# Block-sparse attention scores: both heads of a pair in the two halves of TensorE's rows, the block mask as a product of its own

## The chip, the cores and the metric

The program runs on one core of one Trainium2 chip. The metric is the device time of one execution, in microseconds (us). The engines named below are TensorE (PE in the profile; its weight loads are PEld), VectorE (DVE), ScalarE (ACT), GpSimd (POOL) and the sync engine (SP), which here only issues DMAs.

## What is computed

There are 4 batches, 8 heads, 768 positions and a head size of 64. Every query attends to its own block of 64 keys and to the 3 of the 12 blocks with the highest gate scores, causally. The output of attention, `x` of 768 x 512 per batch, goes through a two-dimensional Fourier transform (the real part is added), a normalisation and a two-layer network.

```python
k_rep = k.reshape(B, H, n_blocks, 64, D).mean(axis=3)
gate_scores = np.where(causal, np.einsum('bhsd,bhnd->bhsn', q, k_rep), -1e9)
top_idx = np.argsort(gate_scores, axis=-1)[..., -3:]
# mask: the 3 blocks of top_idx and the own block, and key position <= query position
scores = np.where(mask, scale * q @ k.T, -1e9)
x = softmax(scores) @ v
...
u = x + real(fft(fft(x, axis=1), axis=2))
un = (u - mean(u)) / sqrt(var(u) + 1e-6)
out = u + relu(un @ w_ch1) @ w_ch2
```

## The kernel before

Heads are taken two at a time: 16 pairs, `kk` from 0 to 15, four to a batch. Queries and keys lie transposed, head size on the partitions, and scores are computed with keys on the partitions and queries along the columns, so that the exp of a score tile is at once the weights of the product with v.

**Stages of a pair.** `stage_A` (called twice by `stage_AA`, first for k, then for q; line 247) transposes 128 x 128 tiles of both heads on TensorE in f32. VectorE copies q to `qt` (line 264) and sums k by blocks into `kr12` (line 270); GpSimd casts each head's q from `qt` into rows 0 to 63 of `qg[e]` (line 267); ScalarE casts each head's k into rows 0 to 63 of `kI[e]` (line 282; for pairs 0 to 6 one of the four casts is VectorE's, line 280). `stage_B` (line 287) computes the gate scores (ten f32 products `g`), then VectorE finds the eight largest of each row (`max`), marks the blocks below the third largest and takes the own block out (lines 294 to 306). `stage_C` (line 308) transposes these marks with five products `gt`, whose weights have 44 columns, and VectorE copies them into rows 64 to 75 of `qg[0]` and `qg[1]`, two copies of 12 x 640. Rows 64 to 75 of `kI[e]` hold a constant, `IndN`: -60000 where the key lies in block n, else 0. So one product over 76 rows gives score plus block mask.

**Sections.** `stage_S(kk, e, s)` (line 334) computes one of three sections of one head's scores: 896 columns in two or three products (the list `SECS`) into `sp`, a tile of two PSUM banks named `sc` with two buffers. For pairs below `EARLY` = 7 it also adds a triangle of -60000 (`ltri`, line 348) to each diagonal tile by a product with the identity; for later pairs VectorE multiplies the result by a 0/1 triangle instead (line 355). ScalarE takes the exp of 896 columns at once into `ptl` (line 349). `stage_AV` (line 357) multiplies with v in 21 products of 65 columns, VectorE divides by the sum into `x` (lines 374 and 375), and for the second head of a pair sums and differences for the transform follow: `fs` on GpSimd (on VectorE for the last pair of a batch), then `ft`, `fo`, `fc` (lines 383 to 407).

**The rest of a batch.** `stage_S1` (products `za`, `ya`, lines 416 to 424) and `stage_S2` (`mx`, lines 448 to 459) transform, `stage_N` normalises, `stage_T` transposes (`unt`, line 506), `stage_M1` (`ha`, `hb`, line 522) and `stage_M2` (`ch`, line 536) are the network; M1 and M2 make up most of TensorE's work.

**The order** of TensorE's and GpSimd's instructions is the order in which the program issues them. It is written out by hand in the loop over pairs (lines 653 to 689): six sections a pair, one after another, each followed by a slot of `filler` and one of the other stages. `filler` takes units of the rest of earlier batches from a queue, by a planner's clock (`feed.now`) in which each unit has a cost: chain units (S1, S2, T) are taken in order, each once the clock stands a given gap past the end of the one before it, bulk units (M1, M2) at any time; line 573 shares the work out evenly. A section advances the clock by at least `PACE` = 1.4. A batch's S1 follows 3.5 after the second `stage_AV` of its fourth pair. VectorE, ScalarE and the DMA queues have their instructions ordered by the compiler's scheduler.

Of the kernel before, what the change touches and what calls it, by code (L numbers as in the profile page):

```python
# [118 lines left out]
def kernel(  # L119
# [9 lines left out]
    nc = tc.nc  # L129
# [55 lines left out]
    kI_t = [[const([128, S], F16, f"kI_{e}_{sl}") for sl in range(3)] for e in range(2)]  # L185
    v16_t = [const([128, 2, NST, 66], F16, f"v16_{sl}") for sl in range(4)]
    qg_t = [[const([128, S], F16, f"qg_{e}_{sl}") for sl in range(3)] for e in range(2)]
    warm = const([128, 512], F16, "warm")
    kr24_t = [const([128, 2 * NB], FP, f"kr24_{sl}") for sl in range(2)]
    gmp_t = [const([128, NST - 1, 2, 32], F16, f"gmp_{sl}") for sl in range(2)]  # L190
# [56 lines left out]
    def stage_A(kk, who, g):  # L247
        d = P[kk]
        src = d["qn"] if who == 0 else d["kn"]
        if who == 0 and g == 0:  # L250
            d["qt"] = apool.tile([128, S], FP, tag="qT32", name=f"qT32_{kk}")
            d["qg"] = [qg_t[e][kk % 3] for e in range(2)]
        if who == 1 and g == 0:
            d["kI"] = [kI_t[e][kk % 3] for e in range(2)]
            d["kr12"] = spool.tile([128, NB], FP, tag="kr12", name=f"kr12_{kk}", bufs=2)
            d["kr24"] = kr24_t[kk % 2]
# [6 lines left out]
        if who == 0:  # L263
            nc.vector.tensor_copy(out=d["qt"][:, cols], in_=flat)  # L264
            if g == 1:
                for e in range(2):
                    nc.gpsimd.tensor_copy(out=d["qg"][e][0:64, :],  # L267
                                          in_=d["qt"][64 * e:64 * e + 64, :])
        else:
# [7 lines left out]
            for e in range(2):  # L277
                dst, src_ = d["kI"][e][0:64, cols], flat[64 * e:64 * e + 64]
                if kk < EARLY and g == 1 and e == 1:
                    nc.vector.tensor_copy(out=dst, in_=src_)  # L280
                else:
                    nc.scalar.copy(out=dst, in_=src_)  # L282
# [4 lines left out]
    def stage_B(kk):  # L287
# [11 lines left out]
        for st in range(NG):  # L299
            for e in range(2):  # L300
                nc.vector.max(out=mx8[:, st, e, :], in_=gsb[:, st, e, :])  # L301
        gm = gmp[:, :, :, 0:NB]
        nc.vector.tensor_tensor(out=gm, in0=gsb,
                                in1=mx8[:, :, :, 2:3].to_broadcast([128, NG, 2, NB]),
                                op=mybir.AluOpType.is_lt)
        nc.vector.tensor_tensor(out=gm, in0=gm, in1=oth24[:, 1:NST, :, :], op=MULT)

    def stage_C(kk):
        d = P[kk]
        gt = pst([44, NG, 128], f"gt_{kk}", dtype=F16)  # L310
        for st in range(NG):
            nc.tensor.transpose(gt[0:44, st, :],  # L312
                                d["gmp"][:, st, :, :].rearrange("p e n -> p (e n)")[:, 0:44], id16)
        for e in range(2):
            nc.vector.tensor_copy(out=d["qg"][e][64:64 + NB, 128:S],
                                  in_=gt[32 * e:32 * e + NB].rearrange("p a c -> p (a c)"))
# [17 lines left out]
    def stage_S(kk, e, s):  # L334
        d = P[kk]
        if s == 0:
            d.setdefault("pt", {})[e] = apool.tile([128, 3 * SEC], F16, tag=f"ptl{e}",
                                                   name=f"ptl_{kk}_{e}")
        pt = d["pt"][e]
        sp = pst([128, 1024], f"sc_{kk}_{e}_{s}", tag="sc", bufs=2)  # L340
        by_pe = kk < EARLY
        for (jt, a0, a1, co) in SECS[s]:
            diag = by_pe and a0 == 128 * jt
            nc.tensor.matmul(sp[:, co:co + (a1 - a0)],  # L344
                             d["kI"][e][0:76, 128 * jt:128 * (jt + 1)],
                             d["qg"][e][0:76, a0:a1], start=True, stop=not diag)
            if diag:
                nc.tensor.matmul(sp[:, co:co + 128], id16, ltri, start=False, stop=True)  # L348
        nc.scalar.activation(out=pt[:, SEC * s:SEC * (s + 1)], in_=sp[:, 0:SEC], func=AF.Exp,  # L349
                             scale=0.125)  # L350
        if s == 2 and not by_pe:
            um = ut01.rearrange("p (o c) -> p o c", o=1).to_broadcast([128, 3, 128])
            for dg in (pt.rearrange("p (t c) -> p t c", t=3)[:, :, 0:128],
                       pt[:, 384:].rearrange("p (t c) -> p t c", t=3)[:, :, 384:512]):
                nc.vector.tensor_tensor(out=dg, in0=dg, in1=um, op=MULT)
# [190 lines left out]
    def queue_batch(b, start):  # L546
        last = start
        units = []
        for dt in (1, 0):
            last = Unit(lambda dt=dt: stage_S1(b, dt), S1_COST, last, 3.5 if dt == 1 else 0.0)  # L550
# [48 lines left out]
    PACE = 1.4  # L599
    with tc.manual_schedule(engines={mybir.EngineType.PE, mybir.EngineType.Pool}):  # L600
# [14 lines left out]
        for sl in range(3):  # L615
            for e in range(2):
                nc.gpsimd.dma_start(kI_t[e][sl][64:64 + NB, :], dr["IndN"].ap())
        nc.gpsimd.dma_start(ut01, dr["ut01"].ap())
        for e in range(2):
            for sl in range(3):  # L620
                nc.gpsimd.memset(qg_t[e][sl][64:64 + NB, 0:128], 0.0)
# [31 lines left out]
        for kk in range(NK):  # L653
            for p in range(6):
                t_in = feed.now
                main(stage_S, 0.39, kk, p // 3, p % 3)
                filler(kk, 2 * p)
                if p == 0 and kk + 2 < NK:
                    load_v(kk + 2)
                    main(stage_AA, 0.7, kk + 2, 1)  # L660
                if p == 1 and kk > 0:
                    main(stage_AV, 0.65, kk - 1, 1)
                    after_av(kk - 1)
                if p == 2:
                    if kk + 2 < NK:
                        main(stage_AA, 0.7, kk + 2, 0)
                        cast_v(kk + 2)
                    if kk == 0:
                        stage_W(4)
# [55 lines left out]
```

## Time and profile before

The times of three runs were 346.15 (median), 346.09 and 347.31 us. One further execution was profiled: it took 346.12 us, 344.3 us from its first to its last instruction (the span).

| | |
|---|---|
| profiled execution, its span | 346.12 us, 344.3 us |
| mean granted TensorE clock | 0.979 |
| ScalarE: exps of sections, line 349 | 96 x 917 ns, 87.1 us busy |
| TensorE: products of sections, line 344 | 256, 55.7 us busy; weight loads 24.5 us |
| TensorE: triangles, line 348 | 84 x 222 ns |
| ScalarE and VectorE: casts of k, lines 282 and 280 | 57 x 473 ns and 7 x 560 ns |
| GpSimd: casts of q, line 267 | 32 x 849 ns |
| VectorE: copies of the marks, line 315 | 32 x 484 ns |
| VectorE: own block out of the marks, line 306 | 16 x 217 ns |
| TensorE: gate products, line 291 | 160 x 271 ns |

A group of the profile is named by line, engine, operation and tiles (out<-in), with its count; busy time counts overlapping instructions once, and the mean is that of one instruction from start to end. TensorE's products overlap, so that the distance of their starts, which the timeline shows, is what one costs in a row of them, not its own length.

### The profile page before, as it was taken

What the parts mean: (1) busy time and instruction counts of PE and PEld (TensorE: products, weight loads), DVE (VectorE), ACT (ScalarE), POOL (GpSimd) and SP (SyncE); (2) the same over time, 40 slices, a digit from 0 to 9 for tenths busy, and PEclk for the clock granted to TensorE, in tenths of its full rate; (3) what the DMA queues carried; (4) which work ended last, traced back from release to release, by engine and by line L of the source; (5) the groups of instructions that cost most, each with busy time, mean ns of one, the idle gap of its engine ahead of it and who ended that gap; (6) DMA issues with size and microseconds to landing.
All of it is one profiled execution on the core that took longest, in us unless ns stands there. A gap on an engine that the chain in (4) does not pass through costs nothing.

```text
span 344.3 us, 6929 instructions
## 1 busy us (share of the span) xinstructions
PE 320.4 (93%) x2688; PEld 210.2 (61%) x2688; DVE 229.1 (67%) x701; ACT 172.7 (50%) x259; POOL 93.5 (27%) x177
## 2 busy tenths in 40 slices
PE   7899994998899989999999989899999999899995
PEld 3577772886766666566566766556666655456442
DVE  2788889788565779887566688986544868533211
ACT  3177885497874853454375653442566210344000
POOL 8435664244543020342215030161012100200000
PEclk9999998799699999999999999999999999999999
DMA  9999999966498440433523000011000011100021
GB/s 173 197 211 208 261 183 219 147 143 138 80 172 144 82 93 17 107 107 89 143 48 74 20 2 30 32 44 51 32 0 2 5 58 61 62 2 0 32 89 64
DMA packets 85312, 31.18 MB, mean 91 GB/s; under 512 B 77736, under 2 KB 81136, under 8 KB 85280
## 3 DMA queue, kind: packets, MB, share of 16 engines
q1 hardware_dynamic: 79984, 25.88, 33.2%
q0 software_dynamic: 3552, 4.40, 8.1%
q10 hardware_dynamic: 1744, 0.46, 0.7%
q8 instruction: 21, 0.34, 0.4%
q14 instruction: 11, 0.09, 0.1%
HBM read 28.63 MB, written 6.29 MB: 101 GB/s over the span
## 4 chain that ended last, share of the span: by engine, by line
PE 74%; DVE 12%; ACT 4%; POOL 4%; issue 3%; DMA 2%; ACTq 0%; POOLq 0%; DVEq 0%
PE ch L536 21%; PE ha L522 15%; PE hb L522 8%; PE sc L344 8%; PE g L291 5%; PE av L370 5%; PE tp L259 3%; ACT kI L282 2%; DVE kr L270 2%; DVE mx L301 2%; DMA qn<-in_q_dram 2%; PE gt L312 1%; PE ya L424 1%; PE mx L448 1%; DVE bst L461 1%
## 5 line engine op out<-in xcount | busy, mean ns | idle before, releaser
L349 ACT ACTIVATE ptl<-sc 128x896 f16<-128x896 f32 x96 | 87.1, 917 | 51.9 <-PE sc L344 42.1
L536 PE MATMUL ch<-w_sb,hT 128*128 128x512 f16 x384 | 91.2, 379 | 1.3 <-DVE u L539 1.2
L522 PEld LDWEIGHTS <-w_sb 128*128 128x128 f16 x512 | 48.8, 98 | 35.7 <-issue 0.7
L522 PE MATMUL ha<-unT,w_sb 128*128 128x512 f16 x256 | 65.7, 379 | 0.1
L344 PE MATMUL sc<-qg,kI 76*128 76x512 f16 (+3 forms) x256 | 55.7, 309 | 4.1 <-ACT ptl L349 4.0
L536 PEld LDWEIGHTS <-hT 128*128 128x128 f16 x384 | 36.1, 97 | 36.8 <-issue 1.4
L525 ACT ACTIVATE hT<-ha 128x512 f16<-128x512 f32 x64 | 38.1, 597 | 30.7 <-PE ha L522 30.7
L527 DVE TENSOR_SCALAR hT<-hb 128x256 f16<-128x256 f32 x64 | 26.9, 422 | 36.1 <-PE hb L522 36.1
L522 PE MATMUL hb<-unT,w_sb 128*128 128x256 f16 x256 | 38.4, 273 | 0.3 <-ACT unT L509 0.3
L383 POOL TENSOR_TENSOR fs<-x 128x384 f16<-128x384 f16 x12 | 11.2, 929 | 100.2 <-DVE x L375 100.2
L344 PEld LDWEIGHTS <-kI 76*128 76x128 f16 x256 | 24.5, 101 | 19.4 <-issue 2.9
L282 ACT CAST kI<-tp 64x384 f16<-64x384 f32 x57 | 27.0, 473 | 11.7 <-DVE kr L270 10.7
L267 POOL CAST qg<-qT 64x768 f16<-64x768 f32 x32 | 27.2, 849 | 19.7 <-DVE qT L264 18.7
L539 DVE TENSOR_TENSOR u<-ch,u 128x512 f32<-128x512 f32 x24 | 16.5, 688 | 21.6 <-PE ch L536 21.3
L370 PE MATMUL av<-v,ptl 128*128 128x65 f16 x672 | 26.2, 195 | 0.0
L370 PEld LDWEIGHTS <-ptl 128*128 128x128 f16 x672 | 24.8, 98 | 2.1 <-issue 0.2
L497 ACT ACTIVATE x<-u,nmr,rstd 128x512 f16<-128x512 f32 x12 | 8.9, 803 | 26.8 <-POOL nmr L490 26.8
L270 DVE TENSOR_REDUCE kr<-tp 128x6 f32<-128x384 f32 x32 | 17.0, 546 | 7.0 <-PE tp L259 6.9
L291 PEld LDWEIGHTS g<-kr,qT 128*128 128x128 f32 x160 | 20.5, 200 | 1.3 <-issue 0.3
L291 PE MATMUL g<-kr,qT 128*128 128x24 f32 x160 | 20.6, 271 | 0.0
L348 PE MATMUL sc<-ltri,id 128*128 128x128 f16 x84 | 18.6, 222 | 0.0
L375 DVE TENSOR_TENSOR x<-av,rcp 128x384 f16<-128x384 f32 x32 | 17.8, 557 | 1.0
(91 smaller groups left out, 406.5 us busy)
## 6 DMA issues: line engine op xcount, KB each, us to landing
vn<-in_v_dram SPq DMA_DIRECT2D x32, 192.0 KB, 3.6
out_dram<-u SPq DMA_DIRECT2D x24, 256.0 KB, 2.0
kn<-in_k_dram SPq DMA_DIRECT2D x30, 192.0 KB, 4.0
qn<-in_q_dram SPq DMA_DIRECT2D x30, 192.0 KB, 4.1
w_sb<-in_moe_w_ch_dram POOLq DMA_DIRECT2D x8, 256.0 KB, 6.9
w_sb<-in_moe_w_ch_dram POOLq DMA_DIRECT2D x4, 512.0 KB, 8.5
cs_sb<-c_CS SPq DMA_DIRECT2D x1, 289.5 KB, 4.8
ss_sb<-c_SS SPq DMA_DIRECT2D x1, 289.5 KB, 3.6
```

What stands on the lines that cost most here:

```text
L267: nc.gpsimd.tensor_copy(out=d["qg"][e][0:64, :], in_=d["qt"][64 * e:64 * e + 64, :])
L270: nc.vector.tensor_reduce(out=d["kr12"][:, 6 * g:6 * g + 6], in_=ps.rearrange("p a (x c) -> p a x c", x=2), axis=mybir.AxisListType.X, op=ADD)
L282: nc.scalar.copy(out=dst, in_=src_)
L291: nc.tensor.matmul(gps[:, st - 1, :], d["qt"][:, 128 * st:128 * (st + 1)], d["kr24"], start=True, stop=True)
L344: nc.tensor.matmul(sp[:, co:co + (a1 - a0)], d["kI"][e][0:76, 128 * jt:128 * (jt + 1)], d["qg"][e][0:76, a0:a1], start=True, stop=not diag)
L348: nc.tensor.matmul(sp[:, co:co + 128], id16, ltri, start=False, stop=True)
L349: nc.scalar.activation(out=pt[:, SEC * s:SEC * (s + 1)], in_=sp[:, 0:SEC], func=AF.Exp, scale=0.125)
L370: nc.tensor.matmul(av[:, st, 0:65], pt[:, o:o + 128], d["v16"][:, e, jt, 0:65], start=(cnt == 0), stop=(cnt == 20))
L522: nc.tensor.matmul(hp_, w1_sb[:, dt, 128 * it:128 * (it + 1)], unT[:, dt, c0:c1], start=(dt == 0), stop=(dt == NDT - 1))
L525: nc.scalar.activation(out=hT[:, c0:c1], in_=hp_, func=AF.Relu)
L527: nc.vector.tensor_scalar(out=hT[:, c0:c1], in0=hp_, scalar1=0.0, scalar2=None, op0=mybir.AluOpType.max)
L536: nc.tensor.matmul(cps, x["hT"][it][:, 128 * st:128 * (st + 1)], w2_sb[:, it, :], start=(it == 0), stop=(it == NIT - 1))
```

## The change

Rows 64 to 75 of `kI` and `qg` disappear. `k16` and `q16` hold both heads of a pair: head 0 on partitions 0 to 63, head 1 on 64 to 127, each filled by one cast of 128 partitions instead of two of 64. The block mask has tiles of its own: `ind` (`IndN` four times, at partitions 0, 32, 64 and 96) and `mk` (the transposed marks of head 0 at partitions 0 and 32, of head 1 at 64 and 96). The multiplication in `stage_B` writes each head's marks twice side by side, so that `stage_C` transposes full tiles of 128 columns and one copy of 128 x 640 fills `mk`.

`stage_S(kk, s)` now does a section of both heads: first the scores, the heads in turn, each over 64 rows; then the mask, over 12 rows, each head and PSUM bank from its own quarter of the rows, and without the first 128 queries, where no block is masked; then, for pairs 0 to 6, the triangles; then both exps. It takes both `sc` buffers.

The loop has three sections a pair with `PACE` = 2.4, and four `filler` slots each. Both `stage_AV` of a pair stand after the first section of the next pair; `stage_C` stands in the second section and `stage_B` in the third. S1 follows the second `stage_AV` by 4.5 in batch 0 and by 6.0 in the others.

```diff
-    kI_t = [[const([128, S], F16, f"kI_{e}_{sl}") for sl in range(3)] for e in range(2)]
+    k16_t = [const([128, S], F16, f"k16_{sl}") for sl in range(3)]
+    q16_t = [const([128, S], F16, f"q16_{sl}") for sl in range(3)]
+    mk_t = [const([128, S - 128], F16, f"mk_{sl}") for sl in range(2)]
+    ind = const([128, S], F16, "ind")
-    qg_t = [[const([128, S], F16, f"qg_{e}_{sl}") for sl in range(3)] for e in range(2)]
-    gmp_t = [const([128, NST - 1, 2, 32], F16, f"gmp_{sl}") for sl in range(2)]
+    gmp_t = [const([128, NST - 1, 2, 2, 32], F16, f"gmp_{sl}") for sl in range(2)]
...
-                for e in range(2):
-                    nc.gpsimd.tensor_copy(out=d["qg"][e][0:64, :],
-                                          in_=d["qt"][64 * e:64 * e + 64, :])
+                nc.gpsimd.tensor_copy(out=d["q16"], in_=d["qt"])
...
-            for e in range(2):
-                dst, src_ = d["kI"][e][0:64, cols], flat[64 * e:64 * e + 64]
-                if kk < EARLY and g == 1 and e == 1:
-                    nc.vector.tensor_copy(out=dst, in_=src_)
-                else:
-                    nc.scalar.copy(out=dst, in_=src_)
+            nc.scalar.copy(out=d["k16"][:, cols], in_=flat)
...
-        gt = pst([44, NG, 128], f"gt_{kk}", dtype=F16)
+        gt = pst([128, NG, 128], f"gt_{kk}", dtype=F16)
         for st in range(NG):
-            nc.tensor.transpose(gt[0:44, st, :],
-                                d["gmp"][:, st, :, :].rearrange("p e n -> p (e n)")[:, 0:44], id16)
-        for e in range(2):
-            nc.vector.tensor_copy(out=d["qg"][e][64:64 + NB, 128:S],
-                                  in_=gt[32 * e:32 * e + NB].rearrange("p a c -> p (a c)"))
+            nc.tensor.transpose(gt[:, st, :], d["gmp"][:, st, :, :, :].rearrange("p e o n -> p (e o n)"),
+                                id16)
+        d["mk"] = mk_t[kk % 2]
+        nc.vector.tensor_copy(out=d["mk"], in_=gt.rearrange("p a c -> p (a c)"))
...
-    def stage_S(kk, e, s):
+    def stage_S(kk, s):
...
+        sp = [pst([128, 1024], f"sc_{kk}_{e}_{s}", tag="sc", bufs=2) for e in range(2)]
...
         for (jt, a0, a1, co) in SECS[s]:
-            diag = by_pe and a0 == 128 * jt
-            nc.tensor.matmul(sp[:, co:co + (a1 - a0)],
-                             d["kI"][e][0:76, 128 * jt:128 * (jt + 1)],
-                             d["qg"][e][0:76, a0:a1], start=True, stop=not diag)
-            if diag:
-                nc.tensor.matmul(sp[:, co:co + 128], id16, ltri, start=False, stop=True)
...
+            for e in range(2):
+                r = slice(64 * e, 64 * e + 64)
+                mm(e, d["k16"][r, 128 * jt:128 * (jt + 1)], d["q16"][r, a0:a1], co, a1 - a0, False)
+        for (jt, a0, a1, co) in SECS[s]:
+            skip = 128 if a0 == 0 else 0
+            for e in range(2):
+                r = slice(64 * e + 32 * (co // 512), 64 * e + 32 * (co // 512) + NB)
+                mm(e, ind[r, 128 * jt:128 * (jt + 1)], d["mk"][r, a0 + skip - 128:a1 - 128],
+                   co + skip, a1 - a0 - skip, not by_pe)
+        if by_pe:
+            for (jt, a0, a1, co) in SECS[s]:
+                if a0 == 128 * jt:
+                    for e in range(2):
+                        mm(e, id16, ltri, co, 128, True)
+        for e in range(2):
+            pt = d["pt"][e]
+            nc.scalar.activation(out=pt[:, SEC * s:SEC * (s + 1)], in_=sp[e][:, 0:SEC], func=AF.Exp,
+                                 scale=0.125)
...
-            last = Unit(lambda dt=dt: stage_S1(b, dt), S1_COST, last, 3.5 if dt == 1 else 0.0)
+            last = Unit(lambda dt=dt: stage_S1(b, dt), S1_COST, last, (4.5 if b == 0 else 6.0) if dt == 1 else 0.0)
...
-    PACE = 1.4
+    PACE = 2.4
...
-        for sl in range(3):
-            for e in range(2):
-                nc.gpsimd.dma_start(kI_t[e][sl][64:64 + NB, :], dr["IndN"].ap())
+        for g in range(4):
+            nc.gpsimd.dma_start(ind[32 * g:32 * g + NB, :], dr["IndN"].ap())
         nc.gpsimd.dma_start(ut01, dr["ut01"].ap())
-        for e in range(2):
-            for sl in range(3):
-                nc.gpsimd.memset(qg_t[e][sl][64:64 + NB, 0:128], 0.0)
...
         for kk in range(NK):
-            for p in range(6):
+            for p in range(3):
                 t_in = feed.now
-                main(stage_S, 0.39, kk, p // 3, p % 3)
-                filler(kk, 2 * p)
+                main(stage_S, 0.6, kk, p)
+                filler(kk, 4 * p)
+                if p < 2 and kk + 2 < NK:
+                    if p == 0:
+                        load_v(kk + 2)
+                    main(stage_AA, 0.7, kk + 2, 1 - p)
+                if p == 1 and kk + 2 < NK:
+                    cast_v(kk + 2)
+                if p == 1 and kk + 4 < NK:
+                    load_qk(kk + 4)
+                filler(kk, 4 * p + 1)
+                if p == 0 and kk > 0:
+                    main(stage_AV, 0.65, kk - 1, 0)
+                if p == 1 and kk + 1 < NK:
+                    main(stage_C, 0.3, kk + 1)
+                filler(kk, 4 * p + 2)
+                if p == 0 and kk > 0:
+                    main(stage_AV, 0.65, kk - 1, 1)
+                    after_av(kk - 1)
+                if p == 2 and kk + 2 < NK:
+                    main(stage_B, 1.05, kk + 2)
+                filler(kk, 4 * p + 3)
...
-                    if kk == 0:
-                        stage_W(4)
```

`stage_W(4)` is four products on constants whose result is not used. In `mm`, the first product into a bank clears it and all later ones add, so the section's products may come in any order of tiles. For pairs from 7 on the triangle of the diagonal stays VectorE's, as before.

## The prediction

> **What bounds the kernel now.** I read the page's totals first, then five stretches, then TensorE's timeline and its waits.
>
> ```profile
> PE 320.4 (93%) x2688; PEld 210.2 (61%) x2688; DVE 229.1 (67%) x701; ACT 172.7 (50%) x259; POOL 93.5 (27%) x177
> ```
>
> ```profile
> 18.00:50.00 32.00, 30.00 (x376) 24.01 (x375) 26.46 (x102) 26.81 (x36) 17.51 (x25) 1.00 1.14 215
> 50.00:68.00 18.00, 12.56 (x138) 10.62 (x136) 15.86 (x51) 9.10 (x14) 6.73 (x12) 0.81 1.03 190
> 68.00:82.00 14.00, 13.60 (x165) 10.92 (x163) 12.60 (x50) 12.60 (x21) 4.74 (x8) 1.00 0.65 137
> 82.00:98.00 16.00, 13.22 (x122) 10.35 (x120) 9.38 (x30) 13.30 (x22) 9.63 (x19) 0.79 0.69 123
> 98.00:345.00 247.00, 236.82 (x1824) 146.16 (x1821) 155.31 (x436) 106.48 (x161) 43.23 (x82) 1.00 0.21 55
> ```
>
> A stretch gives its bounds, its length, then busy time of PE, PEld, DVE, ACT and POOL, and TensorE's clock. From 98 us on, TensorE is busy in 237 of 247 us: what it is spared or given there moves the end one for one. Before 98 us it is not alone: 50 to 68 us loses 18 - 12.6 = 5.4 us idle and, at a clock of 0.81, another 0.19 x 12.6 = 2.4 us; 82 to 98 us loses 2.8 idle and 0.21 x 13.2 = 2.8.
>
> ```profile
> 225.17 0.55 PE L344 MATMUL sc<-qg,kI 76*128 76x512 f16 x3
> 225.56 1.89 PE L536 MATMUL ch<-w_sb,hT 128*128 128x512 f16 x8
> 227.38 0.46 PE L312 MATMUL gt<-id,gmp 128*44 128x128 f16 x5
> 227.77 1.04 PE L536 MATMUL ch<-w_sb,hT 128*128 128x512 f16 x4
> 228.64 0.55 PE L344 MATMUL sc<-qg,kI 76*128 76x512 f16 x3
> 229.02 1.03 PE L536 MATMUL ch<-w_sb,hT 128*128 128x512 f16 x4
> 229.89 0.80 PE L370 MATMUL av<-v,ptl 128*128 128x65 f16 x21
> 230.53 1.02 PE L536 MATMUL ch<-w_sb,hT 128*128 128x512 f16 x4
> ```
>
> Here starts count, not the modelled ends. Four 512-column products take 0.87 us (229.02 to 229.89), some 216 ns each, 2.4 columns a ns: TensorE goes at the pace of its columns, its weight loads hidden. 21 av products take 0.64 us, 30.5 ns each with a load each. One section of scores of one head (896 columns, 373 ns by the pace) takes 0.39 and 0.38 us.
>
> The gt group shows more. Eight ch at 216 ns from 225.56 would end at 227.29; gt starts at 227.38. Five gt at 55.5 ns (the 128-column pace) would end at 227.66; ch goes on at 227.77. Entering and leaving these 44-column weights costs 0.09 + 0.11 = 0.20 us (the 76-row weights of sc show no such pause); with the slower second product on each side (0.01 each, instruction by instruction), I take **0.108 us per change of the array's division**.
>
> **Part 1, the sections of scores.** Before, a section of both heads costs 2 x 0.384 = 0.77 us, and the two gt changes of a pair, spread over its three sections, 0.07: together 0.84. After, a section is:
> - the scores: 896 columns for both heads at once, 0.38, and 0.03 (one av interval) because the second head starts behind the first: 0.41;
> - the mask: per bank 384 to 512 columns, four quarters at once: 0.16 to 0.21, and up to three intervals of 0.03: about 0.24;
> - three changes (whole to halves, halves to quarters, quarters to whole): 3 x 0.108 = 0.32.
>
> This gives 0.97. gt itself is now 128 columns wide, so its changes are gone, already counted. No row shows a change between halves and quarters, nor two products at once. For the change the ends are 0 (a gain is excluded: nothing is removed) and 0.164, the lag of a 128-column product behind its pace (219 - 55); I take 0.10, the gt row rounded down: section 0.95, **+0.11**. Pairs 7 to 15 run where TensorE is the bound: 27 sections, **+3.0 us**; ends 27 x (0.65 - 0.84) = -5.1 and 27 x (1.14 - 0.84) = +8.1. For the overlap the other end is none at all; that is a rival below.
>
> The Trainium skill (TensorEngine Tiling (Array Packing), Key Properties) says that changing the tiling mode, not merely the tile, drains TensorE; it speaks against this change, prices nothing, and the gt row above is what it looks like here. The skill (TensorE: Matmul & The Clock Gate, Measured speedup vs the span model) gives 3.07 times for four tiles of 32 rows at 512 columns; four products at 0.216 would then take an estimated 0.28, against my 0.24, and the sum would be 27 x 0.04 = 1.1 us later. No row of this trace shows it.
>
> **Part 2, the first pairs.** They have no filler. A pair takes 8.0 us, by the gate products on the chain of waits in order of time:
>
> ```profile
> 24.82 1.10 PE g L291 x10
> ...
> 32.84 1.10 PE g L291 x10
> ...
> 37.05 0.82 ACT ptl L349
> ...
> 40.80 1.10 PE g L291 x10
> ```
>
> Before, the two sc buffers alternate: TensorE fills one while ScalarE takes the other. After, one section takes both, its products alternate between the heads, and the second product of the next section waits for the second exp, with all of TensorE's order behind it. From that release to the first exp: scores 0.38, change 0.10, mask 0.24, change 0.10, two triangles 0.11, the lag of a 128-column product 0.22, hand-over 0.04: 1.2 us; then two exps, 0.82 + 0.92 = 1.74. A section takes 2.95 us, a pair 8.9, **+0.9 for each of pairs 0 to 3, +3.6 us**. TensorE's own work (3 x 1.17 + 0.66 x 2 + 0.64 x 2 + 1.1 + 0.28 = 7.5) hides in it. Ends: 0, if the casts spared on ScalarE (below) pay for it, and 4 x 1.5 = +6.
>
> **Part 3, the moved transforms.**
>
> ```profile
> PE za L416 <- POOL dummyp L227: 4.5, 1, 4.5
> PE sc L344 <- ACT ptl L349: 4.0, 7, 0.8
> PE ya L424 <- DVE hT L527: 1.4, 1, 1.4
> PE ya L424 <- DVE qT L264: 1.1, 1, 1.1
> ```
>
> These are TensorE's waits: total, times, longest. The first is batch 0's transform, issued too early: TensorE stands from 56.0 to 60.5 us, and the next groups run at half pace (six za 0.93 instead of 0.50, six ya 0.97 instead of 0.50, av 1.17 instead of 0.64: 1.5 us). The releaser named is not the true one: fo and fc come from VectorE, whose chain needs 8.5 us from the end of the last av (52.1). By the planner's new gaps and costs, worked through unit by unit, this stage follows the first section of pair 5: 8.9 + 1.2 - 3.1 = 7.0 us after that av. The chain is shorter too: one cast (0.56) is gone from VectorE, and while GpSimd cast q twice (0.82 to 1.04 each) three of its steps took 1.1 instead of 0.55; one cast of q is left, so about 0.9 comes back. 8.5 - 0.56 - 0.9 = 7.0. I leave 0.5: **-5.6 us** (ends 0 and -6.1). What is late next is VectorE's copy of q for pair 6 behind the same chain, which the gate products of pair 6 wait for, up to 3.7 us. In batches 1 and 2 the gap 6.0 puts four M1 units and a section before the stage (7.0 us after the av, against 3.6): the pauses between za and ya (starts 120.43 to 122.45 and 202.30 to 204.10, less 0.50 of work: 1.5 and 1.3) go, **-2.8**. For batch 3 the same gap costs: two more M2 units stand before its transform, so four instead of six (16 ch products for 24) cover its normalisation, and TensorE already waits there: **+1.7** (8 x 0.216).
>
> From 82 to 98 us, 5.6 us are lost while batch 0 is normalised. Afterwards the stage before the transposes of x lies a whole section further back, ScalarE has a cast less per pair, but its work for pairs 5 to 7 (exps 15.7, casts 2.9, copies of y, u, x and unT 11.9: 30.5 us) must fit in about 31. I count half as gained, **-2.5** (ends 0 and -5.6).
>
> **Part 4, at nothing.** ScalarE's 57 casts of k at 473 ns become 32; VectorE loses seven at 560 and 16 gt copies at 484, and gains up to 0.22 in 16 gate products of double width; GpSimd loses 16 casts at 849. From 98 us on TensorE covers all that; ahead of it they are in parts 2 and 3. Uncovered, the wider gate product would cost 3.5. Four IndN transfers replace six and six memsets go, on GpSimd before 7 us, which the q transfers cover (first S at 18.0). On SP's queue, v, k and q loads keep their order; the k and q loads follow the same q transposes as before. The four warm-up products left out stood before a wait. The mask now waits for a copy (0.48) after gt, at least a section ahead.
>
> **Sum.** 3.0 + 3.6 - 5.6 - 2.8 + 1.7 - 2.5 = -2.6; profiled execution 346.1 us around a span of 344.3 (median of the runs 346.15, the same): **343.5 us**. My range for this case is 337 to 344.
>
> **Rivals.**
> - *The changes of division decide*, slower: in each section of scores a change costs the 0.164 lag instead of 0.10, and weights that cannot be loaded across a change add another 0.03 each: section 0.95 + 3 x 0.094 = 1.23, 27 x 0.28 = 7.6 us more: 351 us. It outweighs the gains once a section costs over 1.05 us. For it: the gt row shows the load not ahead of its product after a change. Against: that row's total is 0.108. 24%.
> - *The paired exps decide*, slower: ScalarE's row is 917 ns x96, and pairs 4 to 7 also run at 2.95 us or more per section, so parts 3's first and last gains are waits elsewhere (-5.6 to -2, -2.5 to 0): 343.5 + 6.1 = 349.6. Against: VectorE and ScalarE both lose work there. 13%.
> - *No overlap*: halves and quarters run one after another, so the change doesn't do what it says. Scores 0.77, mask 0.64 to 0.75 a section, changes 0.30: 1.78, 0.94 more than before; 27 x 0.94 = 25 instead of 3.0, and 21 early sections with a third hidden another 13: 379 us. That each head and bank has rows of its own speaks against it. 5%.
> - *Nothing to tell*: part 3's gains (10.9) lose a quarter to new waits: 346. 14%.
> - *Changes nearly free* (0.02 each, towards the lower end): section 0.70, 27 x 0.25 = 6.8 us less: 337. 12%.
>
> **How the numbers follow.** This measurement can tell about 0.5%, 1.7 us. Forecast 32%, changes nearly free 12%, nothing to tell 14%, the two slower cases 24 and 13%, no overlap 5%. The first two are faster, the third is the same, the last three are slower: 0.44, 0.14, 0.42. The range leaves out no overlap and the outer tails: 335 to 354.
>
> **What would show it.** Starts in the timeline: a section from its first k16 product to the next group 0.9 to 1.0 us, the second head's product within 0.03 us of the first; gt without the 0.1 us pauses; gate products of the first pairs 8.9 us apart; no 4.5 us wait at the first za and no pause from za to ya; a longer pause before the last transposes of x. Sections over 1.05 us, or a TensorE wait on the exps beyond pair 4, would make the forecast wrong.

## The result, and the profile after

The changed kernel takes 359.82 us (median of four runs, 357.47 to 363.90) against 346.12 (345.88 to 347.31) for the kernel before: ratio 1.037, 95% interval 1.029 to 1.045, slower. Repeated in a later set it took 361.63 against 346.87, ratio 1.042 (1.040 to 1.045). Executions over 1.5% above the fastest of their kernel are left out of all ratios, so a median can lie above its ratio times the time before, and the profile shown here is that of the repeated run (361.02 us), since the first run's was of such an execution (363.90 us).

Totals of the changed kernel:

```profile
span 358.9 us, 7330 instructions
PE 336.4 (94%) x2940; PEld 208.5 (58%) x2940; DVE 215.6 (60%) x678; ACT 157.6 (44%) x234; POOL 78.4 (22%) x153
```

VectorE, ScalarE and GpSimd lost 13 to 15 us of work each. TensorE, meant to be spared, is busy 16 us longer. The same five stretches as before (bounds, length, busy PE, PEld, DVE, ACT, POOL, then TensorE's clock):

```profile
18.00:50.00 32.00, 29.20 (x314) 19.74 (x315) 16.99 (x71) 17.82 (x24) 11.43 (x16) 0.82 0.90 187
50.00:68.00 18.00, 15.82 (x201) 11.48 (x199) 13.41 (x43) 11.13 (x16) 5.50 (x8) 0.88 0.96 182
68.00:82.00 14.00, 13.58 (x145) 10.98 (x146) 9.69 (x32) 7.71 (x12) 6.57 (x11) 0.76 0.77 140
82.00:98.00 16.00, 15.42 (x176) 11.29 (x176) 12.12 (x46) 10.96 (x16) 7.03 (x18) 0.92 0.53 120
98.00:359.00 261.00, 247.53 (x2037) 146.58 (x2034) 154.63 (x447) 106.51 (x162) 39.79 (x78) 0.98 0.22 56
```

Look at the clock column. Before, it was 1.00 from 18 to 50 us and from 68 to 82; now it is 0.82 and 0.76. Busy time says nothing of it: a slow clock makes products longer, and the engine looks busier. The chain of waits (start, length, engine and line) shows the first pairs:

```profile
21.53 1.15 PE sc L349 x12
22.70 1.74 ACT ptl L370 x2
24.47 1.14 PE sc L349 x7
25.64 1.73 ACT ptl L370 x2
27.42 1.88 PE sc L349 x11
29.29 1.28 PE tp L263 x6
30.57 2.31 PE av L391 x42
32.88 1.28 PE sc L349 x7
```

The section from 21.53 to 24.47 takes 2.94 us, products and two exps in turn. The next takes 2.95, to 27.42. In the third the products alone take 1.88, then six transposes take 1.28 (0.66 at full clock) and 42 av 2.31 (1.28): the clock has fallen, and it is 5.5 us from the start of this section (27.42) to that of the next one (32.88).

A section in the filled part, from the timeline:

```profile
237.75 1.03 PE L557 MATMUL ch<-w_sb,hT 128*128 128x512 f16 x4
238.71 0.55 PE L349 MATMUL sc<-q,k 64*128 64x512 f16 x4
239.19 0.39 PE L349 MATMUL sc<-mk,ind 12*128 12x512 f16 x4
239.51 1.04 PE L557 MATMUL ch<-w_sb,hT 128*128 128x512 f16 x4
```

Four ch from 237.75 end by the pace at 238.61; 0.10 us for the change into halves, 0.48 until the mask, 0.32 until the next ch: 0.90 us. TensorE's waits (total, times, longest):

```profile
PE sc L349 <- ACT ptl L370: 4.3, 11, 0.4
PE unt L527 <- DVE x L396: 2.0, 1, 2.0
PE unt L527 <- DVE x L514: 2.0, 1, 2.0
PE g L288 <- DVE qT L268: 1.4, 1, 1.4
```

The 4.5 us at the first za and the pauses before ya are gone; in their place stand the exps, two waits at transposes (unt, batches 0 and 3) and the gate products.

**Where the time went**, from the starts of first exps and first products in the two traces. At its first ha the changed kernel has already done more work on pairs 7 to 10: 12 transposes, ten gate products, five gt and three sections, 5.0 us by what they take in the kernel before. These 5.0 us are taken off the time after in the fourth row and off the time before in the fifth. Differences are taken before rounding.

| stretch | before, us | after, us | difference | predicted |
|---|---|---|---|---|
| start to first exp of pair 0 | 18.7 | 19.8 | +1.1 (18.3 to 20.2 over all kernels) | 0 |
| first exp of pair 0 to that of pair 4 | 31.7 | 41.3 | +9.6 | +3.6 |
| pair 4 to pair 7 | 42.2 | 38.4 | -3.8 | -5.6 |
| pair 7 to the first ha | 3.0 | 6.2 | +3.3 | -2.5 |
| first ha to the end | 243.8 | 248.2 | +4.4 | +1.9 |
| sum | | | +14.6 | -2.6 |

### The profile page after: what moved, and what is told of

Read it like the earlier page. It is cut to its first block, busy times and chain, and to the rows that moved or that the text cites. A ratio compares the mean times of both kernels' runs of the same rounds, so it can differ in the third digit from the quotient of the medians.

```text
span 362.1 us, 7330 instructions
## 1 busy us (share of the span) xinstructions
PE 339.3 (94%) x2940; PEld 211.1 (58%) x2940; DVE 216.4 (60%) x678; ACT 157.6 (44%) x234; POOL 78.4 (22%) x153
## 4 chain that ended last, share of the span: by engine, by line
PE 74%; DVE 13%; ACT 6%; POOL 3%; issue 2%; DMA 1%; ACTq 0%; POOLq 0%; DVEq 0%
PE ch L557 21%; PE ha L543 15%; PE sc L349 11%; PE hb L543 7%; PE av L391 5%; PE g L288 4%; ACT ptl L370 4%; PE tp L263 4%; PE unt L527 2%; DMA qn<-in_q_dram 1%; DVE ft L410 1%; PE za L437 1%; DVE x L396 1%; PE ya L445 1%; PE mx L469 1%
## 5 line engine op out<-in xcount | busy, mean ns | idle before, releaser
L370 ACT ACTIVATE ptl<-sc 128x896 f16<-128x896 f32 x96 | 82.8, 915 | 81.6 <-PE sc L349 81.6
L557 PE MATMUL ch<-w_sb,hT 128*128 128x512 f16 x384 | 89.8, 379 | 1.6 <-ACT hT L546 1.6
L543 PE MATMUL ha<-unT,w_sb 128*128 128x512 f16 x256 | 67.6, 387 | 1.7 <-DVE hT L548 1.7
L349 PE MATMUL sc<-q,k 64*128 64x512 f16 (+3 forms) x256 | 32.7, 324 | 4.4 <-ACT ptl L370 4.3
L391 PEld LDWEIGHTS <-ptl 128*128 128x128 f16 x672 | 25.8, 102 | 2.8 <-issue 0.3
L349 PEld LDWEIGHTS <-k 64*128 64x128 f16 x256 | 10.4, 96 | 21.4 <-issue 16.2
L349 PE MATMUL sc<-mk,ind 12*128 12x384 f16 (+3 forms) x256 | 19.4, 327 | 0.0
L268 DVE COPY qT<-tp 128x384 f32<-128x384 f32 x32 | 16.6, 548 | 4.5 <-PE tp L263 4.5
L279 ACT CAST k<-tp 128x384 f16<-128x384 f32 x32 | 14.6, 485 | 10.6 <-DVE kr L272 10.4
L263 PE MATMUL tp<-id,kn 128*128 128x128 f32 x96 | 18.8, 345 | 0.2 <-DVE u L560 0.2
```

Of the source, the lines that this page charges most:

```text
L263: nc.tensor.transpose(ps[:, i, :], src[:, 3 * g + i, :, :].rearrange("p h d -> p (h d)"), id32)
L349: nc.tensor.matmul(sp[e][:, co:co + n], lhsT, rhs, start=bank not in first, stop=last, skip_group_check=True)
L391: nc.tensor.matmul(av[:, st, 0:65], pt[:, o:o + 128], d["v16"][:, e, jt, 0:65], start=(cnt == 0), stop=(cnt == 20))
L543: nc.tensor.matmul(hp_, w1_sb[:, dt, 128 * it:128 * (it + 1)], unT[:, dt, c0:c1], start=(dt == 0), stop=(dt == NDT - 1))
L557: nc.tensor.matmul(cps, x["hT"][it][:, 128 * st:128 * (st + 1)], w2_sb[:, it, :], start=(it == 0), stop=(it == NIT - 1))
```

## The experiments

Three theories were set up first. A: both score buffers held by one section leave TensorE waiting for the second exp, and the waiting drops its clock. B: the changes of division cost. C: the moved stages and gaps cost. The kernels of the table are explained below it, in their groups; every time stands beside the median of the kernel before in the same set of runs, and the last two columns are read from the one execution that was profiled, whose time is given.

| kernel | median, before, us | ratio (95%) | profiled, us | us per pair, 0 to 3 | clock 18 to 50 us |
|---|---|---|---|---|---|
| before |  |  | 346.1 | 7.92 | 1.00 |
| changed, repeated | 361.6, 346.9 | 1.042 (1.040-1.045) | 361.0 | 10.32 | 0.82 |
| warm products of 128 rows | 360.5, 347.4 | 1.039 (1.032-1.045) | 358.0 | 9.12 | 1.00 |
| 76 rows, by head | 349.1, 347.4 | 1.008 (1.004-1.011) | 351.9 | 7.70 | 1.00 |
| 76 rows, in turn | 356.3, 347.4 | 1.016 (1.009-1.022) | 359.2 | 9.53 | 0.84 |
| the same again | 356.9, 347.3 | 1.018 (1.011-1.024) | 351.1 | 8.40 | 1.00 |
| gaps alone | 351.9, 347.4 | 1.013 (1.010-1.017) | 351.1 | 8.00 | 0.96 |
| changed, gaps back | 360.3, 346.3 | 1.041 (1.037-1.045) | 360.3 | 10.38 | 0.84 |
| divided in pairs 8 to 15 only | 349.4, 346.9 | 1.009 (1.005-1.012) | 348.8 | 7.92 | 1.00 |
| the same, gaps back, gt wide | 342.6, 346.3 | 0.994 (0.990-0.997) | 342.2 | 7.71 | 1.00 |
| before with gt wide | 344.9, 346.9 | 0.994 (0.991-0.996) | 345.5 | 7.88 | 0.95 |
| the same, gap 6.0 in batches 1, 2 | 345.4, 346.9 | 0.996 (0.994-0.999) | 345.1 | 7.71 | 1.00 |
| changed, early sections by head | 378.8, 347.3 | 1.064 (1.058-1.071) | 379.3 | 13.15 | 0.61 |
| warm products of 12 rows | 370.8, 347.0 | 1.066 (1.063-1.070) | 370.8 | 10.75 | 0.84 |
| warm products of 76 rows | 365.8, 347.0 | 1.053 (1.048-1.058) | 363.1 | 9.12 | 1.00 |
| early by head, warm 128 rows | 371.3, 347.0 | 1.069 (1.065-1.073) | 376.3 | 11.72 | 1.00 |

**The first four: clock, buffers, gaps.** The changed kernel with three unused products of 128 rows after the second and third section of pairs 0 to 6:

```diff
                 filler(kk, 4 * p + 3)
+                if kk < 7 and p > 0:
+                    stage_W(3)
```

> The changed kernel with three products on constants added after the second and third section of pairs 0 to 6, where TensorE stood waiting for the second exp (their result is not used). Theory A, the paired buffers leave TensorE idle and the idle drops its clock: the clock of 18 to 68 us rises from 0.86 to over 0.95, a pair falls from 10.6 us to about 9.0, the whole from 359.8 to about 350. Theory A without the clock, the waits alone cost: no change within 2 us. Theory B, the changes of the array's division cost: 42 more products of 0.216 us, so up to 9 us slower.

Its clock is 1.00 until 82 us, pairs fall from 10.3 to 9.1 us, the first za comes 7.3 us earlier (65.1 for 72.4). Theory A expected the clock and the pairs so, but a time of about 350 us, and that missed: of the 7.3 us the trace has 4.8 left at the first exp of pair 7 (94.6 for 99.5) and 3.0 at the end, and by their ratios the two kernels can't be told apart. Its chain of waits, where batch 0 is normalised:

```profile
89.82 0.33 POOL nmr L511
90.14 0.02 issue
90.17 2.22 ACT x L518 x3
92.39 0.81 ACT ptl L370
93.20 0.04 issue
93.24 1.34 PE sc L349 x8
```

On ScalarE the exp of a section (92.39) follows three activations of x that waited for GpSimd's `nmr`, and TensorE, which has given both score buffers away, waits 4.4 us for it. So what is gained in the first pairs is lost in the stage after them. That this wait, too, comes from holding both buffers is argued here, not tested.

The changed order and gaps with the products of before, heads one after another (by head), and the same with heads in turn:

```diff
+    def stage_SS(kk, s):
+        for e in range(2):
+            stage_S(kk, e, s)
...
-                main(stage_S, 0.39, kk, p // 3, p % 3)
+                main(stage_SS, 0.6, kk, p)
```

```diff
+        for (jt, a0, a1, co) in SECS[s]:
+            for e in range(2):
+                mm(e, d["kI"][e][0:76, 128 * jt:128 * (jt + 1)], d["qg"][e][0:76, a0:a1], co,
+                   a1 - a0, not by_pe)
```

> The products of before (76 rows, array undivided) in the loop of the change: three slots a pair, both av together, gaps 4.5 and 6.0; in a section all products of head 0, then all of head 1. Theory A: head 0's buffer is filled again while head 1's exp runs, so early pairs take about 8.2 us, the clock stays up, 343 to 347 us in all. Theory B says the same, as nothing is divided. Theory C, the moved stages and gaps cost: about 360, like the change.

> The same as the kernel by heads, but the heads' products in turn within a section, and the triangles after them, as in the change; nothing divided. Theory A: TensorE waits for the second exp behind one product of head 0 in the early sections; from that release to the next exp 0.9 us (the change: 1.2), so a section 2.7 us and a pair 8 to 8.5 at full clock, up to 10 where the clock drops; 2 to 8 us slower than by heads. Theory B: the same time as by heads within 1 us.

By head, the whole new order costs 0.8% (349.1 us, where theory A expected 343 to 347 and theory C about 360) and its pairs are as short as those of the kernels with the old order (7.70; there 7.71 to 8.00). In turn, with no change to the division of the rows, it costs 1.6%, and its four executions lie from 351.2 to 359.2 us. So it was run again:

> The products of 76 rows with the heads in turn once more, unchanged, because its first four runs lay from 351.2 to 359.2 us. Its pairs show what holding both score buffers costs without any division of the rows. Theory A: an undisturbed profile again shows pairs 0 to 3 at 9.0 to 9.6 us against 7.70 by head, TensorE's clock under 0.9 from 18 to 50 us, and the time lies at 352 to 357, 3 to 8 above the kernel by head (349.1). If the first runs were a mishap, the pairs take 7.7 to 8.0 and the time is within 1 us of 349.

The stretch from 18 to 50 us, first in the execution profiled here (351.12 us), then in the one that was profiled the first time (359.21 us); and the waits on the exps in the same order:

```profile
18.00:50.00 32.00, 28.14 (x341) 22.14 (x339) 25.99 (x94) 24.10 (x35) 16.51 (x24) 1.00 1.09 205
18.00:50.00 32.00, 28.63 (x292) 23.04 (x291) 22.41 (x88) 21.85 (x31) 13.94 (x19) 0.84 0.95 194
```

```profile
PE sc L368 <- ACT ptl L383: 5.0, 13, 0.4
PE sc L368 <- ACT ptl L383: 4.4, 12, 0.4
```

Three things follow. Where the clock stays 1.00, holding both buffers costs 8.40 - 7.70 = 0.70 us a pair by itself. Second, the clock of this kernel differs from one execution to another: 1.00 with pairs of 8.40 us, or 0.84 with pairs of 9.53, with waits on the exps of 0.4 us at most in both and nothing divided in its sections. So such waits can go with a low clock where the sections hold no narrow products, as theory A has it, but they don't in every execution. The changed kernel (11 waits, 4.3 us, 0.4 at most) had 0.85 and 0.82 in its two profiles, and 0.84 with the gaps put back; what its narrow products add is left to the last experiments. Third, from its first ha to its end this kernel takes 245.3 and 245.7 us in the two traces; the changed kernel, with the same order, the same gaps and the same work ahead of its first ha, takes 248.2. By the sections alone (0.90 us against 0.84, 23 of them) that is 1.4; the rest goes with longer waits for hT, 3.4 us against 1.9 and 1.0.

The kernel before with the new gaps alone, `(4.5 if b == 0 else 6.0)` for 3.5:

> The kernel before with the gaps of the change alone (4.5 for batch 0, 6.0 for the others). If the gaps do what the prediction said: the 4.5 us wait ahead of batch 0's transform shrinks by about 1 us (it moves by one section only), the pauses between za and ya of batches 1 and 2 go (-2.8), the pause ahead of the last transposes grows by 1.7: 343 to 345 us. Theory C, the gaps cost: over 348.

```profile
PE unt L506 <- DVE x L493: 4.1, 2, 2.2
PE za L416 <- POOL dummyp L227: 3.4, 1, 3.4
```

The gaps cost 1.3%. The wait at the first za shrinks to 3.4, as expected, but the waits for x at its transposes grow from 0.8 to 4.1 us. In the changed kernel, the old gap put back:

> The changed kernel with the gap of before (3.5) ahead of every S1; all else as changed. The prediction counted the gaps as a gain of 5.6 + 2.8 - 1.7 = 6.7 us: if that were so, this run is 361.6 + 6.7 = 368 us. If the gaps cost in this order what they cost alone in the kernel before (351.9 - 347.4 = 4.5), it is 357. If they only move a wait from one stage to the next, it stays at 361.6 within 1.5. I hold the last, since batch 0's transform is followed in this order by the gate products of pair 6, which wait for VectorE behind the same chain.

It stays at ratio 1.041: there the gaps neither gain nor cost more than about 1 us; a wait only changes its place.

**Repeat, late division, wide gt.** The changed kernel itself, then divided sections and new order only from pair 8 on, with the new gaps:

```diff
+    HY = 8
...
+            if kk >= HY:
+                nc.scalar.copy(out=d["k16"][:, cols], in_=flat)
+                return
```

> The changed kernel once more, on the chip of the runs beside it: 357 to 362 us. Its undisturbed profile should show 10 us a pair for pairs 0 to 3, sections of 0.90 us from start to start in the filled part, and the clock under 0.9 before 100 us.

The repeat came as expected, 361.6 us with 10.32 us a pair and sections of 0.90 us, but for the clock from 82 to 98 us, which was 0.92.

> Pairs 0 to 7 with the products and the order of before, pairs 8 to 15 with the divided rows and the order of the change; the gaps of the change throughout (4.5 and 6.0), so it stands beside the kernel with these gaps alone (351.9 us, first M1 at 99.5 us of 349.1). Theory A, the loss lies in the early pairs: first M1 within 1 us of that kernel, 24 sections at 0.06 us more, in all 1 to 3 us above 351.9. Theory B, the divided sections themselves cost: 5 us or more above it.

Against the gaps alone (1.013) this is 1.009, where 1 to 3 us more were expected: 24 divided sections on TensorE's critical stretch cost little. From the first ha to the end it takes 250.2 us against 249.6; the first ha comes 2.7 us earlier (96.8 for 99.5), ahead of any divided section. Then the one part of the change that spares a division, gt over 128 columns, in the kernel before:

```diff
-        gt = pst([44, NG, 128], f"gt_{kk}", dtype=F16)
+        gt = pst([128, NG, 128], f"gt_{kk}", dtype=F16)
...
-                                  in_=gt[32 * e:32 * e + NB].rearrange("p a c -> p (a c)"))
+                                  in_=gt[64 * e:64 * e + NB].rearrange("p a c -> p (a c)"))
```

> The kernel before with the marks transposed as full tiles of 128 columns, nothing else (one buffer of double width for the marks instead of two). If a change of the array's division costs 0.1 us as the trace of before has it, the two around each of 16 groups of gt go: 16 x 0.2 = 3.2 us of TensorE's time, of which pairs 8 to 15 count in full: 1.7 to 3.2 us faster, 343 to 344.5 on a chip where before takes 346. If the 0.1 us is something else that lay around gt: no change.

> The wide marks, and the gap 6.0 for batches 1 and 2 alone (3.5 as before for 0 and 3). If the pauses between za and ya of these two batches go without a price elsewhere: another 1 to 2.8 us below the wide kernel, 341 to 343 where before takes 346. If the gap itself is what made the kernel with the gaps alone slow: no faster than the wide kernel.

It gains 0.6%, and its trace has the pauses gone: 216 ns from the start of the last ch to that of the first gt where before had 309, and 56 from the last gt to the next ch where before had 151. 32 changes of division at about 0.1 us are 3.2 us; about 2 (346.9 to 344.9) are found, what the 18 of them in pairs 7 to 15 come to. A gap of 6.0 for batches 1 and 2 adds nothing. Wide gt, old gaps and divided late pairs together:

> Pairs 0 to 7 as before but with gt transposed as 128 full columns, pairs 8 to 15 with the divided rows and the changed order, every S1 gap as before (3.5). By the sections alone (0.90 us against 0.77 where gt no longer divides, 24 of them): 344.9 + 24 x 0.13 = 348 us. If the changed order of the late pairs pays for its divided sections, as the comparison of the kernel with divided late pairs (349.4) and the one with the gaps alone (351.9) suggests (2.5 less instead of 1.4 more), it is 344 to 345. Theory A (all of the loss lies in pairs 0 to 7) holds if it is under 349; a cost of the divisions in the filled part (theory B) shows as 350 or more.

```profile
82.00:98.00 16.00, 13.19 (x141) 9.54 (x139) 11.63 (x37) 13.06 (x21) 11.75 (x23) 1.00 0.77 140
```

Its median, 342.6 us, is the shortest of all, but its ratio is that of gt wide alone, so the two can't be told apart. Its eleven executions lie at 342.1 to 342.6 (six, mean clock 0.99) and at 344.1 to 346.9 (five, 0.975 to 0.98); the profiled one is of the first group. From its first ha (91.9) to its end (340.4) it takes 248.5 us; gt wide alone takes 247.0 (96.5 to 343.5). So 24 divided sections cost about 1.5 us there, 0.06 each, where 0.13 was expected; in this execution more than that comes back ahead of the first ha, where the clock is 1.00 from 82 to 98 us (0.79 before). Theory B falls as the main cause: in the filled part the division costs 0.6 to 2.9 us by these two comparisons and that with the kernel in turn, and most of the loss lies in pairs 0 to 7 and what follows from them.

**What drops the clock.** The changed kernel, but pairs 0 to 7 issue scores, mask, triangles and exp of head 0, then of head 1, on the same divided rows:

```diff
-        for (jt, a0, a1, co) in SECS[s]:
-            for e in range(2):
...
+        for es in ([[0], [1]] if kk < 8 else [[0, 1]]):
             for (jt, a0, a1, co) in SECS[s]:
...
+                for e in es:
```

> The changed kernel, but pairs 0 to 7 issue each section head by head: scores, mask, triangles and exp of head 0, then of head 1, with the same divided rows; so the heads no longer overlap in TensorE (it works longer: 2 x (0.37 + 0.21 + 0.3 + 0.11) = 2.0 us a section instead of 1.17, a pair 7.5 + 2.5 = 10 us), but one score buffer can be filled while the exp of the other runs. Theory A, that the loss is the idle time of TensorE and the clock that falls with it: TensorE is then busy all the time, its clock 1.00 from 18 to 50 us, pairs at 9.5 to 10 us, and the time 1 to 3 us under the changed kernel (361.6), although it does 20 us more work in these 24 sections. If the overlap of the heads were worth what it spares TensorE, the time would be 10 to 20 us above the changed kernel, 372 to 380.

Theory A missed on the clock, the pairs and the time, and in an instructive way: the profiled execution (379.25 us) has no TensorE wait from 18 to 50 us at all, and a clock of 0.61. The eight executions lie from 368.2 to 385.1 us with mean clocks from 0.958 down to 0.905, so 0.61 is what one of the longer ones had. Its stretch, and its timeline:

```profile
18.00:50.00 32.00, 32.00 (x205) 17.94 (x204) 11.90 (x55) 14.16 (x18) 5.81 (x7) 0.61 0.64 134
```

```profile
28.26 0.92 PE L349 MATMUL sc<-q,k 64*128 64x512 f16 x2
29.12 0.60 PE L349 MATMUL sc<-mk,ind 12*128 12x512 f16 x2
29.66 0.39 PE L349 MATMUL sc<-ltri,id 128*128 128x128 f16 x2
29.98 0.92 PE L349 MATMUL sc<-q,k 64*128 64x512 f16 x2
```

896 columns take 0.86 us (28.26 to 29.12), half pace, with the next group always ready. Hence theory D: products over few rows count for the clock like waiting. Three runs test it: the unused products of the first experiment, now over 12 and over 76 rows (the three just ahead of the loop over pairs likewise), and those of 128 rows in the kernel with early sections by head:

```diff
-                nc.tensor.matmul(wps, warm[:, 0:128], warm, start=True, stop=True)
+                nc.tensor.matmul(wps, warm[0:rows, 0:128], warm[0:rows], start=True, stop=True)
```

> The changed kernel with the three unused products of 512 columns after the second and third section of pairs 0 to 6, as in the run with warm products, but over 12 rows instead of 128, so they take the same columns (and two changes of division, 0.1 each). Theory A as it stood, that waiting drops TensorE's clock: they fill the same waits, so the clock from 18 to 50 us is 1.00 as there and a pair takes 9.1 to 9.4. New theory D, after the run with the sections of pairs 0 to 7 head by head (TensorE without a pause from 20 to 33 us, its clock half all along): the clock follows how much of the array's rows the products use, waits and narrow products alike; then 12 rows warm nothing, the clock stays at 0.75 to 0.88 and pairs take over 10 us.

> The same with 76 rows, which need no change of division. Theory D with rows counted: 76 of 128 rows warm partly, the clock from 18 to 50 us lies between that of the run with 12 rows and 1.00; if what counts is whether the whole array is addressed (no division), it is 1.00 and a pair 8.9 to 9.1, as with 128 rows. Theory A as it stood expects 1.00 too.

> The kernel with pairs 0 to 7 head by head (378.8, TensorE's clock 0.61 from 18 to 50 us with no pause) plus the three unused products of 128 rows after the second and third section of pairs 0 to 6. They add 7 x 6 x 0.216 = 9 us of work to a TensorE that already has no pause. Theory D: the clock rises above 0.8 from 18 to 50 us, a pair takes under 12.5 us instead of 13.15 although it does 1.3 us more. Theory A as it stood (only waiting drops it) has nothing to fill here: clock 0.6, a pair 13.15 + 2.1 = 15 us.

The stretch from 18 to 50 us with 12 rows, with 76 rows, and by head with 128 rows:

```profile
18.00:50.00 32.00, 31.28 (x329) 20.86 (x326) 17.39 (x75) 17.82 (x24) 11.49 (x16) 0.84 0.85 184
```

```profile
18.00:50.00 32.00, 31.28 (x404) 21.43 (x405) 19.97 (x79) 21.97 (x30) 12.78 (x18) 1.00 1.06 204
```

```profile
18.00:50.00 32.00, 32.00 (x313) 18.78 (x314) 15.63 (x66) 19.18 (x24) 10.83 (x15) 1.00 0.84 179
```

In the first two TensorE waits for the same time, 0.7 us in two waits on the exps and none behind them, and is busy for 31.28 us; only the rows of the unused products differ, with the two changes of division that 12 rows need, and the clock is 0.84 or 1.00. All executions agree in the direction: the mean clock of a whole execution is 0.926 to 0.943 with 12 rows, 0.948 to 0.965 with 76. So filling the waits with narrow products doesn't lift the clock, and with wide ones it does: theory D holds, and A as it stood, which expected 1.00 for both, is not the whole. The third (376.31 us, again one of the longer executions) adds 9 us of work to a TensorE without pauses: pairs become shorter, 11.72 for 13.15, and every execution of it has a higher mean clock (0.963 to 0.985) than any without the products (0.905 to 0.958). In time the ratios (1.069 and 1.064) don't differ by more than their intervals: the work is paid for by the clock, no more. Whether rows or the divided mode itself count stays open: no run used few rows without a division.

## Why the prediction was wrong

From -2.6 to +14.6 us the prediction is 17.2 us off. By the table of stretches 6.0 of this lie in pairs 0 to 3, 1.8 in pairs 4 to 6, 5.8 between pair 7 and the first ha, 2.5 behind it, and 1.1 ahead of the first exp.

**Part 2, the step that failed first.** "A section takes 2.95 us, a pair 8.9, +0.9 for each of pairs 0 to 3, +3.6 us". The wait for the second exp was right, and its size where the clock is full: 2.94 us from 21.53 to 24.47; with the clock brought to 1.00 by wide products in the waits, a pair takes 9.12 us for the 8.9 of the prediction. The step that failed is "TensorE's own work ... 7.5 hides in it", which took TensorE's clock as full throughout. It was 0.82, and a pair took 10.32: +2.4 a pair, +9.6 for the four. By steps: 7.70 with the new order by head, 8.40 with both buffers held and the clock at 1.00, and between that and 10.32 the divided sections' longer way to the exp together with the clock; wide products in the waits return 1.2 of it, their own 1.3 us of work included. What lowers the clock is shown in part: narrow products don't keep it up, and with waits of 0.4 us it was low without them in one of two executions. How much of the 0.82 is due to each stays open.

**Part 1, right.** Predicted 0.95 us a section, measured 0.90; 0.84 before. The change of division taken at 0.10 is 0.10 at the entry. The second head starts 3 to 4 ns behind the first, and the four quarters of the mask within 10 ns, not one av interval (0.03) each. The Trainium skill (TensorE: Matmul & The Clock Gate, The mechanism) gives about 4 ns between the starts of products in different row groups; the trace agrees. So +1.6 for 27 sections instead of +3.0. The rival *changes of division decide* falls: no section reached 1.05 us. *No overlap* and *changes nearly free* fall with the same lines.

**Part 3, half right.** The first za no longer waits 4.5 us, and za to ya no longer pauses. But of 5.6 us, 3.8 arrive by pair 7; "what is late next", the copy of q for pair 6, makes the gate products wait 1.4. The gain of 2.5 while batch 0 is normalised ("I count half as gained") became a loss of 3.3, the second step that failed: TensorE waits 2.0 us at the transposes of batch 0, and its clock is 0.85 from 99.5 to 110.7 us. The experiment with the gaps alone shows the wait at these transposes without any new product (2.2 us, and the kernel 1.3% slower); with the gaps put back in the changed kernel nothing returns, so the gaps don't explain the loss there. Why it is lost beyond the wait and the clock stays open. In batches 1 and 2, the pauses of 2.8 us go, and three waits for hT of 0.9 to 1.6 us come, which the sum didn't have. The cost at batch 3, +1.7, is in the 2.0 us wait of unt for x (0.5 before).

**Part 4** put the engines' own work at nothing; but for the wait of the gate products, named as what would be late next, and those for hT no trace speaks against it.

**The rivals.** *The paired exps decide* (349.6) named the mechanism for the first pairs, and TensorE does wait on exps beyond pair 4, which the prediction had put down as the sign that it was wrong; but behind the first exp of pair 4 (61.04) these are two waits, 0.8 us in all. It held the clock constant too, and was 10 us short. No rival had the clock in it, although the profile of before showed it fall to 0.81 and 0.79 in the two stretches where TensorE paused.

The Trainium skill (TensorE: Matmul & The Clock Gate, A second HAM failure mode: psum-queue depth-cycling) describes a kernel in which short pauses between groups that cycle through PSUM make the clock go up and down. The changed kernel shows the like, 0.82 with waits on the exps of 0.4 us at most. So does the kernel with 76 rows in turn in one of its two profiles (0.84), while in the other the clock stayed 1.00 with the same waits.

## What to carry to other kernels

Before making TensorE's work narrower in a stretch that waits for another engine, read the granted clock there and ask what keeps it up: work spared in such a stretch may be paid back at half pace. Interleaving two outputs that take all buffers of a tile class makes TensorE wait for the consumer of both (here 0.70 us a pair with the clock at 1.00). Put such a change where other work fills the gaps: divided sections in pairs 8 to 15 alone, with wide gt, lose nothing against wide gt alone (both 0.994 of the time before), and gain nothing that shows. And read the clock of more than one execution: that of one kernel was 1.00 or 0.84 in the same stretch.

## What was unexpected of the hardware

- The clock follows more than whether TensorE has something to do: where three products of 512 columns over 12 rows filled the waits it was 0.84, over 76 or 128 rows 1.00; and in one execution with no wait at all from 18 to 50 us, narrow products ran at a clock of 0.61.
- Waits of 0.4 us once a section, with 76-row products, went with a clock of 1.00 in one execution of a kernel and of 0.84 in another.
- Products in different halves of the rows start 3 to 4 ns apart, and four in different quarters within 10 ns.
- A transpose with 44 columns of weights costs 0.1 us at its start and again at its end, as much as a change of division does: with 128 columns both are gone, and the kernel before is 0.6% faster.
